# Two matmul layers on one Trainium2 core: x2 of the state rows kept in SBUF, their products moved into the same chunk, and weight-block sums moved from GpSimd to VectorE

## The chip, the core and the metric

One Trainium2 chip, one of its cores. A time is microseconds on the device for one execution; the figure of a kernel is the median of its runs. The engines are TensorE (PE, with its weight loads PEld), VectorE (DVE), ScalarE (ACT) and GpSimd (POOL); SyncE (SP) issues every DMA of this kernel. Each engine works through its own queue in order and waits at semaphores for the others.

## The reference

Inputs are `x` (8 x 8 x 512 x 64) and `state` (8 x 8 x 32 x 64), both float32, and the weights of two layers; the four weight matrices are float64.

```python
# attention both ways, per batch and head
a  = softmax(scale * x @ state.T);   xread = a @ state      # 512 rows per batch
a2 = softmax(scale * state @ x.T);   sread = a2 @ x         # 32 rows per batch: the state rows
x  = concatenate([xread, sread], axis=2)                    # 8 * (512 + 32) = 4352 rows of 512
# first layer: 512 -> 1024 -> 512
h  = x @ w_in;  solu = h * softmax(h);  ln = (solu - mean) / sqrt(var + 1e-6) * g_ln
x2 = ln @ w_out
# second layer: 512 -> 2048 -> 512
h  = x2 @ w_in2;  g = maximum(0.01 * h, h);  out = g @ w_out2
```

## The kernel before

**Precision.** A float32 product is three products of rounded halves: high x high, high x low, low x high. `mm3` (L99) issues them, `split` (L106) makes the halves: ACT rounds the source to the high half, DVE or POOL subtracts it to get the low half. Weights arrive as float64 words and are narrowed by `narrow` (L151): one ACT step (absolute value, L156) and four DVE steps (L157, L158, L161, L164).

**First layer.** Batches 0 to 7 are the 512 rows each of xread; "batch 8" (B) is the 256 state rows of all batches, in two row blocks. For each batch the program does attention, `h1` and `solu_norm` (normalisation), transposes (`tr`, L406) and `x2` (L426), whose result goes by ACT into the buffer `xo` (one buffer) and by DMA to DRAM (`xs`).

**Second layer.** The 2048 features are cut into 8 chunks of 256, the batches into 4 pairs; `second` (L731) walks pair by pair, chunk by chunk. Within a pair `h2` (L625) computes a chunk's hidden values of both batches with seven products instead of eight (block sums S1 to S4 of the weights, differences T1 to T4 of x2), held in three PSUM accumulators X, Z, Y; ACT and DVE combine them, apply the leaky step and split them into `gb` or `gc`. `out2` (L657) multiplies by the second weights. Its call for chunk c stands in the turn of chunk c + 1.
In pair 0 the weights are split once by `split_chunk` (L503), written to DRAM (`w2s`, `wo2s`), and loaded back by the later pairs. For the first weights POOL makes two subtractions of 128x1024 (L510, L521) and the four sums of 128x256 (L516 to L519). The raw words of the next chunk are loaded as soon as DVE has read the old ones.
The state rows go along with pair 0 only: `h8` (L691) their hidden values, `out8` (L708) their output. Their x2 is written to `xs[8]`, loaded back into the tile `misc` (L678), split there (L683), and h8 and out8 of chunk c are issued in the turn of chunk c + 1, the last in the first turn of pair 1.

**What sets the order.** The program text (`PROGRAM`, L815, and `second`) is only a priority: a scheduler places each instruction in its engine's queue by an estimate of its own of when operands, buffers and engines are free. So an edit in one place moves instructions around it on all engines. Buffers are named by tag: the tag `t4` has four rows of 128x1024, which the narrowed weights, the sums and the normalised rows share; `w` has two buffers, which hold the two halves of w_out until the state rows' x2 is done, and then `misc` and the weights of odd chunks.

Of the kernel before, what the change touches and what calls it, by code (L numbers as in the profile page):

```python
# [10 lines left out]
F32 = mybir.dt.float32  # L11
# [4 lines left out]
ALU = mybir.AluOpType  # L16
# [4 lines left out]
P = 128  # L21
# [12 lines left out]
def f32(ap):  # L34
    return ap.bitcast(F32)
# [3 lines left out]
def attn_solu_leaky_kernel(  # L39
# [15 lines left out]
    nc = tc.nc  # L55
    B, H, S, D = x.shape
# [7 lines left out]
    ND = DM // P  # L64
    NF2 = FF2 // P
    ROWS = S + NS
    HALF = 2 * P
# [5 lines left out]
    dr = ctx.enter_context(tc.tile_pool(name="dr", bufs=1, space=DRAM))  # L73

    def slot(tag, shape, dtype, name, bufs=1):
        return sb.tile(shape, dtype, tag=tag, name=name, bufs=bufs)

    def bank(name):
        return ps.tile([P, 512], F32, tag="p1", name=name, bufs=4)
# [14 lines left out]
        return slot("t4", [P, 1024], F32, name, bufs=4)  # L94


    xs = [dr.tile([P, ND, S if j < B else HALF], F32, name=f"xs{j}") for j in range(B + 1)]

    def mm3(o, ah, al, bh, bl, start, stop, more=False):  # L99

# [5 lines left out]
    def split(hi, lo, src):  # L106
        nc.scalar.copy(hi, src)
        nc.vector.tensor_tensor(lo, src, f32(hi), ALU.subtract)  # L108
# [297 lines left out]
    def tr(b, r):  # L406
# [8 lines left out]
        for u in range(NF // 4):  # L415
# [7 lines left out]
            c = slice(r * P, (r + 1) * P)  # L423
            split(t[0][:, 4 * u : 4 * u + 4, c], t[1][:, 4 * u : 4 * u + 4, c], v)

    def x2(b, u):  # L426
        t = ln_t[b]
        pt = bank(f"x2_{b}_{u}")
        nd = 1 if b < B else 2
        nt = S if b < B else HALF  # L430
        for j in range(nd):
            d = slice((nd * u + j) * P, (nd * u + j + 1) * P)
            for f in range(NF):
                mm3(
                    pt[:, j * nt : (j + 1) * nt],
                    w_out_hi[:, f, d], w_out_lo[:, f, d], t[0][:, f, :], t[1][:, f, :],
                    start=(f == 0), stop=(f == NF - 1),
                )
        o = slot("xo", [P, nd, nt], F32, f"xo{b}_{u}", bufs=1)
        nc.scalar.copy(o, pt.rearrange("p (j t) -> p j t", j=nd))  # L440
        nc.sync.dma_start(xs[b][:, nd * u : nd * (u + 1), :], o)

# [25 lines left out]
    def misc():  # L470
        if "misc" not in ph2:
            ph2["misc"] = slot("w", [P, 2, 2, 1024], F32R, "misc", bufs=2)
        return ph2["misc"]

    def w2_tile(p, c):
        w2[p, c] = slot(
            "w" if c % 2 else "sw0", [P, 2, 2, 1024], F32R, f"w2_{p}_{c}", bufs=2 if c % 2 else 1
        )
        return w2[p, c]
# [23 lines left out]
    def split_chunk(c, kind):  # L503
        w = narrow(ph2["raw"][:, kind], f"wn{c}_{kind}")
        if c < NC - 1:
            load_chunk(c + 1, kind)
        if kind == 0:
            t = w2_tile(0, c)
            nc.scalar.copy(t[:, 0, 0], w)
            nc.gpsimd.tensor_tensor(t[:, 0, 1], w, f32(t[:, 0, 0]), ALU.subtract)  # L510
            sm_ = row(f"ws{c}")
            s_ = [sm_[:, i * 256 : (i + 1) * 256].rearrange("p (k f) -> p k f", k=2) for i in range(4)]
            v = w.rearrange("p (h k g f) -> p h g k f", h=2, k=2, g=2)
            a11, a12, a21, a22 = v[:, 0, 0], v[:, 1, 0], v[:, 0, 1], v[:, 1, 1]
            tt = nc.gpsimd.tensor_tensor
            tt(s_[0], a21, a22, ALU.add)  # L516
            tt(s_[1], s_[0], a11, ALU.subtract)
            tt(s_[2], a11, a21, ALU.subtract)
            tt(s_[3], a12, s_[1], ALU.subtract)  # L519
            nc.scalar.copy(t[:, 1, 0], sm_)  # L520
            nc.gpsimd.tensor_tensor(t[:, 1, 1], sm_, f32(t[:, 1, 0]), ALU.subtract)  # L521
            nc.sync.dma_start(w2s[c], f32(t))
        else:
            t = wo2_tile(0, c)
            nc.scalar.copy(t[:, 0], w)
            nc.gpsimd.tensor_tensor(t[:, 1], w, f32(t[:, 0]), ALU.subtract)
            nc.sync.dma_start(wo2s[c], f32(t))
# [97 lines left out]
    def h2(p, c, part, between=None):  # L625
        C = late("C")[:, c % 2]
        g = gtile(c)
        if part == 0:
            hq[p, c] = [bank1(t, f"h{t}{p}_{c}") for t in "XZY"]
        X, Z, Y = hq[p, c]  # L630
        tt = nc.vector.tensor_tensor
        if part == 0:
            prod(X, p, c, "A11", "B11", True)
            nc.scalar.copy(C[:, 0, 0], X)
            prod(Z, p, c, "A12", "B21", True)
            tt(C[:, 0, 0], C[:, 0, 0], Z, ALU.add)  # L636
            prod(X, p, c, "S2", "T2", False)
            nc.scalar.copy(C[:, 1, 0], X)  # L638
            prod(Y, p, c, "S1", "T1", True)
            if between is not None:  # L640
                h8(between)
            prod(X, p, c, "S3", "T3", False)
            nc.scalar.copy(C[:, 1, 1], X)  # L643
            tt(C[:, 1, 1], C[:, 1, 1], Y, ALU.add)  # L644
            leaky(C[:, 0, 0], C[:, 0, 0])
        else:
            prod(X, p, c, "A22", "T4", False)
            leaky(C[:, 0, 1], X)
            nc.scalar.copy(g[:, 0, 0], C[:, 0])
            nc.gpsimd.tensor_tensor(g[:, 1, 0], C[:, 0], f32(g[:, 0, 0]), ALU.subtract)  # L650
            prod(Y, p, c, "S4", "B22", False)
            tt(C[:, 1, 0], C[:, 1, 0], Y, ALU.add)
            leaky(C[:, 1], C[:, 1])
            nc.scalar.copy(g[:, 0, 1], C[:, 1])
            nc.gpsimd.tensor_tensor(g[:, 1, 1], C[:, 1], f32(g[:, 0, 1]), ALU.subtract)

    def out2(p, c, j, rs=(0, 1, 2, 3)):  # L657
        g = gtile(c)
        o = late("oacc")[:, j]
        w = wo2[p, c].rearrange("p h (f d) -> p h f d", f=2)  # L660
        for r in rs:
            t = slice(r * P, (r + 1) * P)
            pt = bank(f"o{p}_{c}_{j}_{r}")
            for f in range(2):
                mm3(
                    pt, g[:, 0, j, f, t], g[:, 1, j, f, t], w[:, 0, f, :], w[:, 1, f, :],
                    start=(f == 0), stop=(f == 1),
                )
            if c == 0:
                nc.scalar.copy(o[:, r, :], pt)  # L670
            else:
                nc.vector.tensor_tensor(o[:, r, :], o[:, r, :], pt, ALU.add)  # L672
            if c == NC - 1:
                rows = out.rearrange("(b t) d -> b t d", t=ROWS)[2 * p + j, :S, :]
                nc.sync.dma_start(rows.rearrange("(p r) d -> p r d", r=NR)[:, r], o[:, r, :])


    def load_x8():  # L678
        nc.sync.dma_start(
            f32(misc()[:, 1, 1]).rearrange("p (k t) -> p k t", k=ND), xs[B]  # L680
        )

    def split_x8():  # L683
        t = misc()[:, 1]
        nc.scalar.copy(t[:, 0], f32(t[:, 1]))
        nc.vector.tensor_tensor(t[:, 1], f32(t[:, 1]), f32(t[:, 0]), ALU.subtract)

    o8 = {}
    g8 = {}
# [41 lines left out]
    def second():  # L731
        ps2.close()
        psb[0] = ctx.enter_context(tc.tile_pool(name="psc", bufs=1, space=PSUM))

        seq = [(p, c) for p in range(NPAIR) for c in range(NC)]
        for i, (p, c) in enumerate(seq):
            prev = seq[i - 1] if i else None
            new = seq[i + 1] if i + 1 < len(seq) else None
            turn = c == NC - 1 and p < NPAIR - 1
            if new and new[0] == 0:  # L740
                split_chunk(c + 1, 0)
            elif new:
                load_w2(*new)
            if turn:
                load_x2(p + 1)
            if not i:
                h2(p, c, 0)
                x2(B, 0)
                h2(p, c, 1)
                x2(B, 1)  # L750
                load_x8()
                split_x8()
                split_chunk(1, 1)
                out2(p, c, 0)
                out2(p, c, 1)
                continue
            h2(p, c, 0, prev[1] if prev[0] == 0 else None)
            if turn:
                diff_x2(p + 1)
                swap_x2("B11", "B21")  # L760
            if i > 1:
                out2(*prev, 0)
            if turn:
                swap_x2("T2")
            h2(p, c, 1)
            if turn:
                swap_x2("T1", "T3")
            if i > 1:
                out2(*prev, 1)
            if turn:  # L770
                swap_x2("T4", "B22")
            if prev[0] == 0:
                out8(prev[1])
            if new and new[0] == 0:
                split_chunk(c + 1, 1)
            elif new:
                load_wo2(*new)
        out2(*seq[-1], 0)
        out2(*seq[-1], 1)
# [66 lines left out]
```

## Time and profile before

| | |
|---|---|
| median of 3 runs | 1186.05 us (1185.74 to 1187.06) |
| the profiled execution | 1186.7 us |
| its span, first to last instruction | 1184.9 us |
| mean granted clock of PE | 0.983 |
| PE busy | 1126.2 us, 95% |
| DVE, ACT, POOL busy | 648.0, 528.5, 348.8 us |
| chain of waits that ended last | PE 83%, DVE 7%, POOL 3%, issue 3%, ACT 2%, DMA 2% |

The second layer starts at 457 us. A row of the timeline has its start, its duration, the engine, the line, the operation with its tiles, and in brackets how long the engine stood idle before it and who released it. A matmul's duration covers more than its share of the engine, since matmuls overlap: the pace is read from start to start.

### The profile page before, as it was taken

What the parts mean: (1) busy time and instruction counts of PE and PEld (TensorE: products, weight loads), DVE (VectorE), ACT (ScalarE), POOL (GpSimd) and SP (SyncE); (2) the same over time, 40 slices, a digit from 0 to 9 for tenths busy, and PEclk for the clock granted to TensorE, in tenths of its full rate; (3) what the DMA queues carried; (4) which work ended last, traced back from release to release, by engine and by line L of the source; (5) the groups of instructions that cost most, each with busy time, mean ns of one, the idle gap of its engine ahead of it and who ended that gap; (6) DMA issues with size and microseconds to landing.
All of it is one profiled execution on the core that took longest, in us unless ns stands there. A gap on an engine that the chain in (4) does not pass through costs nothing.

```text
span 1184.9 us, 14523 instructions
## 1 busy us (share of the span) xinstructions
PE 1126.2 (95%) x5648; PEld 896.7 (76%) x5648; DVE 648.0 (55%) x1015; ACT 528.5 (45%) x811; POOL 348.8 (29%) x241
## 2 busy tenths in 40 slices
PE   4659999999999998989999999999999999999998
PEld 2347677677768867768888888888888888888887
DVE  6988667675675587456665632334723336323434
ACT  3655646655565444554444434233342325342331
POOL 1241112111102032587775222122231313222221
PEclk8869999999999999999999999999999999999999
DMA  9302202202011225646543574435562534634331
GB/s 293 109 1 56 54 30 54 62 13 63 27 54 63 100 113 186 240 152 256 196 169 151 204 273 149 173 119 201 214 247 108 188 132 165 225 139 182 115 134 71
DMA packets 66444, 162.42 MB, mean 137 GB/s; under 512 B 39624, under 2 KB 39624, under 8 KB 57672
## 3 DMA queue, kind: packets, MB, share of 16 engines
q1 hardware_dynamic: 66376, 161.50, 39.2%
q8 instruction: 44, 0.72, 0.2%
q14 instruction: 24, 0.20, 0.1%
HBM read 118.49 MB, written 42.99 MB: 136 GB/s over the span
## 4 chain that ended last, share of the span: by engine, by line
PE 83%; DVE 7%; POOL 3%; issue 3%; ACT 2%; DMA 2%; SPq 1%; POOLq 0%; ACTq 0%; DVEq 0%
PE o L102 10%; PE o L104 10%; PE o L103 10%; PE x L102 5%; PE hX L103 5%; PE hX L104 5%; PE hX L102 5%; PE x L103 5%; PE x L104 5%; PE h L102 3%; PE h L103 3%; PE h L104 3%; PE hY L104 2%; PE hY L102 2%; PE hY L103 2%
## 5 line engine op out<-in xcount | busy, mean ns | idle before, releaser
L672 DVE TENSOR_TENSOR oacc<-oacc,o 128x512 f32<-128x512 f32 x224 | 151.7, 684 | 104.3 <-PE o L104 104.0
L102 PE MATMUL x<-ln,w_out_hi 128*128 128x512 f32 (+1 forms) x288 | 111.3, 387 | 0.9 <-ACT xo L440 0.9
L103 PE MATMUL x<-ln,w_out_hi 128*128 128x512 f32 (+1 forms) x288 | 109.1, 379 | 0.6 <-DVE r L246 0.3
L104 PE MATMUL x<-ln,w_out_lo 128*128 128x512 f32 (+1 forms) x288 | 109.0, 378 | 0.0
L650 POOL TENSOR_TENSOR gc<-C,gc 128x1024 fp32r<-128x1024 f32 x16 | 42.9, 2684 | 197.8 <-issue 141.6
L104 PE MATMUL o<-wo,gb 128*128 128x512 f32 x256 | 99.7, 389 | 0.0
L104 PE MATMUL o<-misc,gc 128*128 128x512 f32 x256 | 99.7, 389 | 0.0
L103 PE MATMUL o<-wo,gb 128*128 128x512 f32 x256 | 99.7, 389 | 0.0
L102 PE MATMUL o<-wo,gb 128*128 128x512 f32 x256 | 99.7, 389 | 0.0
L103 PE MATMUL o<-misc,gc 128*128 128x512 f32 x256 | 99.6, 389 | 0.0
L102 PE MATMUL o<-misc,gc 128*128 128x512 f32 x256 | 99.6, 389 | 0.0
L650 POOL TENSOR_TENSOR gb<-C,gb 128x1024 fp32r<-128x1024 f32 x16 | 40.5, 2533 | 185.3 <-issue 164.8
L598 ACT ACTIVATE C<-C 128x512 f32<-128x512 f32 x64 | 54.1, 846 | 68.3 <-DVE C L636 40.9
L598 ACT ACTIVATE C<-hX 128x512 f32<-128x512 f32 x32 | 19.1, 598 | 145.1 <-PE hX L104 145.0
L102 PE MATMUL hX<-xbT,w 128*128 128x512 f32 x192 | 75.2, 392 | 2.8 <-ACT C L638 1.6
L103 PE MATMUL hX<-xbT,w 128*128 128x512 f32 x192 | 74.9, 390 | 0.0
L104 PE MATMUL hX<-xbT,w 128*128 128x512 f32 x192 | 74.7, 389 | 0.0
L644 DVE TENSOR_TENSOR C<-C,hY 128x512 f32<-128x512 f32 x32 | 21.9, 685 | 93.2 <-ACT C L643 93.2
L102 PEld LDWEIGHTS x<-ln,w_out_hi 128*128 128x128 f32 x288 | 54.2, 188 | 18.1 <-issue 1.9
L102 PE MATMUL h<-sw,a1T 128*128 128x512 f32 x128 | 54.9, 429 | 11.6 <-DVE cf(0, 0)_446 L362 7.9
L636 DVE TENSOR_TENSOR C<-C,hZ 128x512 f32<-128x512 f32 x32 | 22.0, 686 | 77.0 <-PE hZ L104 72.6
L103 PEld LDWEIGHTS x<-ln,w_out_hi 128*128 128x128 f32 x288 | 54.3, 188 | 11.1 <-DVE ln L108 0.9
(718 smaller groups left out, 2711.2 us busy)
## 6 DMA issues: line engine op xcount, KB each, us to landing
w<-w2s SPq DMA_DIRECT2D x24, 2048.0 KB, 7.9
w2s<-w SPq DMA_DIRECT2D x8, 2048.0 KB, 6.8
wo<-wo2s SPq DMA_DIRECT2D x12, 1024.0 KB, 6.8
misc<-wo2s SPq DMA_DIRECT2D x12, 1024.0 KB, 7.1
xs<-xo SPq DMA_DIRECT2D x34, 256.0 KB, 2.4
out<-oacc SPq DMA_DIRECT2D x34, 256.0 KB, 4.9
xn<-in_x SPq DMA_DIRECT2D x32, 256.0 KB, 4.8
raw<-in_moe_w_in SPq DMA_DIRECT2D x8, 1024.0 KB, 5.2
```

What stands on the lines that cost most here:

```text
L102: nc.tensor.matmul(o, ah, bh, start=start, stop=False, **kw)
L103: nc.tensor.matmul(o, ah, bl, start=False, stop=False, **kw)
L104: nc.tensor.matmul(o, al, bh, start=False, stop=stop, **kw)
L598: nc.scalar.activation(o, v, AF.Lrelu)
L636: tt(C[:, 0, 0], C[:, 0, 0], Z, ALU.add)
L644: tt(C[:, 1, 1], C[:, 1, 1], Y, ALU.add)
L650: nc.gpsimd.tensor_tensor(g[:, 1, 0], C[:, 0], f32(g[:, 0, 0]), ALU.subtract)
L672: nc.vector.tensor_tensor(o[:, r, :], o[:, r, :], pt, ALU.add)
```

## The change

1. x2 of the state rows is no longer written to DRAM: ACT copies both halves of it into a tile `x8f` in SBUF (tag `g8`), and `split_x8` splits it from there into `misc`. The load `load_x8` and the tensor `xs[8]` are gone.
2. h8 and out8 of a chunk are issued in the turn of that same chunk: in chunk 0 between and after the two halves of out2, in chunks 1 to 7 in the middle of h2 and at the turn's end. The last ones no longer stand in pair 1.
3. The four sums of each first-weight chunk are made on DVE; the subtractions stay on POOL.

```diff
-    xs = [dr.tile([P, ND, S if j < B else HALF], F32, name=f"xs{j}") for j in range(B + 1)]
+    xs = [dr.tile([P, ND, S], F32, name=f"xs{j}") for j in range(B)]
...
+    x8 = {}
+
     def x2(b, u):
...
-        o = slot("xo", [P, nd, nt], F32, f"xo{b}_{u}", bufs=1)
-        nc.scalar.copy(o, pt.rearrange("p (j t) -> p j t", j=nd))
-        nc.sync.dma_start(xs[b][:, nd * u : nd * (u + 1), :], o)
+        if b == B:
+            if u == 0:
+                x8["f"] = slot("g8", [P, 2, 512], F32, "x8f")
+            nc.scalar.copy(x8["f"][:, u], pt)
+            return
+        o = slot("xo", [P, S], F32, f"xo{b}_{u}", bufs=1)
+        nc.scalar.copy(o, pt)
+        nc.sync.dma_start(xs[b][:, u, :], o)
...
-            tt = nc.gpsimd.tensor_tensor
+            tt = nc.vector.tensor_tensor
             tt(s_[0], a21, a22, ALU.add)
...
-    def load_x8():
-        nc.sync.dma_start(
-            f32(misc()[:, 1, 1]).rearrange("p (k t) -> p k t", k=ND), xs[B]
-        )
-
     def split_x8():
         t = misc()[:, 1]
-        nc.scalar.copy(t[:, 0], f32(t[:, 1]))
-        nc.vector.tensor_tensor(t[:, 1], f32(t[:, 1]), f32(t[:, 0]), ALU.subtract)
+        v = x8["f"].rearrange("p u c -> p (u c)")
+        split(t[:, 0], t[:, 1], v)
...
                 x2(B, 1)
-                load_x8()
                 split_x8()
                 split_chunk(1, 1)
                 out2(p, c, 0)
+                h8(0)
                 out2(p, c, 1)
+                out8(0)
                 continue
-            h2(p, c, 0, prev[1] if prev[0] == 0 else None)
+            h2(p, c, 0, c if p == 0 else None)
...
-            if prev[0] == 0:
-                out8(prev[1])
+            if p == 0:
+                out8(c)
```

What the scheduler makes of it. The line numbers of the changed kernel are 5 to 7 higher from `x2` on. Up to the split of chunk 0 the queues are the same.

DVE's queue where the state rows' first layer ends, before: `wn0_1` and `wn1_0` are narrowed weights (chunk, first or second weights), `e(8, 1)` the second row block's normalised values, `ln8` the low halves after its transposes, `C` and `hZ` hidden values of chunk 0.

```order
L164 SCALAR_TENSOR_TENSOR wn0_1_3815<-raw_3666,wn0_1_3815 128x1024
L376 TENSOR_SCALAR e(8, 1)_3798<-e(8, 1)_3798,c2(8, 1)_3812 128x1024
L158 TENSOR_SCALAR wn1_0_3977<-wn1_0_3977 128x1024
L161 SCALAR_TENSOR_TENSOR wn1_0_3977<-raw_3666,wn1_0_3977 128x1024
L108 TENSOR_TENSOR ln8_3916<-tr8_0_0_3917,ln8_3916 128x4x128
L108 TENSOR_TENSOR ln8_3916<-tr8_0_1_3924,ln8_3916 128x4x128
L164 SCALAR_TENSOR_TENSOR wn1_0_3977<-raw_3666,wn1_0_3977 128x1024
L157 TENSOR_SCALAR wn1_1_4162<-wn1_1_4162 128x1024
```

And now, with the sums `ws1` of chunk 1:

```order
L164 SCALAR_TENSOR_TENSOR wn0_1_3814<-raw_3665,wn0_1_3814 128x1024
L376 TENSOR_SCALAR e(8, 1)_3797<-e(8, 1)_3797,c2(8, 1)_3811 128x1024
L108 TENSOR_TENSOR ln8_3915<-tr8_0_0_3916,ln8_3915 128x4x128
L108 TENSOR_TENSOR ln8_3915<-tr8_0_1_3923,ln8_3915 128x4x128
L158 TENSOR_SCALAR wn1_0_3976<-wn1_0_3976 128x1024
L161 SCALAR_TENSOR_TENSOR wn1_0_3976<-raw_3665,wn1_0_3976 128x1024
L164 SCALAR_TENSOR_TENSOR wn1_0_3976<-raw_3665,wn1_0_3976 128x1024
L523 TENSOR_TENSOR ws1_3986<-wn1_0_3976 128x256
L525 TENSOR_TENSOR ws1_3986<-wn1_0_3976 128x256
L524 TENSOR_TENSOR ws1_3986<-ws1_3986,wn1_0_3976 128x256
L157 TENSOR_SCALAR wn1_1_4157<-wn1_1_4157 128x1024
```

The two subtractions of the first row block moved ahead of two steps of the narrowing, and the sums follow its last step.

ACT's queue at the same place is nearly unchanged; this is how it stands now (`wn1_1` the absolute value of chunk 1's second weights, `xo7_2` a copy of x2 of batch 7, `hX0_0` the copy of chunk 0's first product):

```order
L532 CAST wo2_0_0_3821<-wn0_1_3814 128x1024
L156 ACTIVATE wn1_1_4157<-raw_3665 128x1024
L447 COPY xo7_2_3955<-x2_7_2_3930 128x512
L107 CAST ln8_3915<-tr8_1_0_3958 128x4x128
L107 CAST ln8_3915<-tr8_1_1_3965 128x4x128
L641 COPY C_3696<-hX0_0_3995 128x512
```

Before, the copy of batch 7 stood behind that of `hX0_0`; the absolute value stood ahead of the casts as it does now.

DVE's queue at the end of chunk 0, now: `ws2` are the sums of chunk 2, `misc` with `x8f` the low half of the state rows' x2.

```order
L659 TENSOR_TENSOR C_3696<-C_3696,hY0_0_3997 128x512
L523 TENSOR_TENSOR ws2_4289<-wn2_0_4279 128x256
L525 TENSOR_TENSOR ws2_4289<-wn2_0_4279 128x256
L524 TENSOR_TENSOR ws2_4289<-ws2_4289,wn2_0_4279 128x256
L526 TENSOR_TENSOR ws2_4289<-wn2_0_4279,ws2_4289 128x256
L108 TENSOR_TENSOR misc_4154<-x8f_4083,misc_4154 128x1024
L157 TENSOR_SCALAR wn2_1_4402<-wn2_1_4402 128x1024
```

Before, nine rows stood between that C and the subtraction of x2: the narrowing of two weights and the first sum of chunk 1's hidden values; now only the four sums stand between. The first sum waits for POOL, which subtracts the high half from the narrowed weights of chunk 1: their row of `t4` becomes `ws2`. On PE, h8 of chunk 0 moved from behind chunk 1's first four products to behind the first 24 matmuls of chunk 0's outputs, and out8 of chunk 0 from chunk 2's start to chunk 1's.

## Rows read from the trace of the kernel before

**Rows 1.** Page, part 4, shares of the span by engine.

```profile
PE 83%; DVE 7%; POOL 3%; issue 3%; ACT 2%; DMA 2%; SPq 1%; POOLq 0%; ACTq 0%; DVEq 0%
```

**Rows 2.** Table by stretches: length, busy us (instructions) per engine, clock, DMA share, GB/s.

```profile
446.00:480.00 34.00, 29.70 (x172) 25.88 (x171) 21.62 (x24) 17.00 (x23) 12.51 (x9) 0.95 0.55 186
480.00:545.00 65.00, 56.52 (x259) 45.70 (x258) 37.12 (x37) 33.94 (x46) 48.45 (x26) 0.97 0.60 223
545.00:1176.00 631.00, 631.00 (x2851) 525.15 (x2850) 275.97 (x368) 234.21 (x308) 200.45 (x90) 1.00 0.46 170
```

**Rows 3.** Timeline of PE, 446 to 545 us: matmuls it waited for.

```profile
447.06 0.50 PE L102 MATMUL x<-ln,w_out_hi 128*128 128x512 f32 x1 [0.92 <-ACT xo L440]
456.82 0.66 PE L419 MATMUL tr<-ident,e(8, 1)_3798 128*128 128x128 f32 x4 [2.99 <-DVE ln L108]
495.00 0.50 PE L102 MATMUL hX<-xbT,w 128*128 128x512 f32 x1 [1.21 <-ACT C L634]
499.60 0.39 PE L103 MATMUL h<-misc,w 128*128 128x256 f32 x1 [1.46 <-DVE misc L686]
506.20 0.50 PE L104 MATMUL hZ<-xbB,w 128*128 128x512 f32 x1 [1.70 <-POOL w L510]
512.76 0.72 PE L104 MATMUL o<-wo,g 128*128 128x512 f32 x1 [2.03 <-POOL g L706]
525.52 0.50 PE L102 MATMUL hX<-xbT,w 128*128 128x512 f32 x1 [1.64 <-ACT C L638]
```

**Rows 4.** Table by stretches, 514 to 516 us, behind two of the gaps.

```profile
514.00:516.00 2.00, 2.00 (x6) 1.52 (x6) 1.52 (x2) 1.20 (x2) 2.00 (x2) 0.50 0.00 0
```

**Rows 5.** Timeline of PE without a gap: start to start.

```profile
464.40 0.39 PE L102 MATMUL hX<-xbT,w 128*128 128x512 f32 x1
465.76 0.28 PE L102 MATMUL x<-ln,w_out_hi 128*128 128x256 f32 x1
...
471.51 0.40 PE L102 MATMUL hX<-xbT,w 128*128 128x512 f32 x1
```

**Rows 6.** Timeline of DVE and POOL, 525 to 533 us.

```profile
525.96 1.23 DVE L161 SCALAR_TENSOR_TENSOR wn<-raw,wn 128x1024 uint32<-128x1024 uint32 x1
527.22 3.31 DVE L164 SCALAR_TENSOR_TENSOR wn<-raw,wn 128x1024 uint32<-128x1024 uint32 x1
...
529.41 3.39 POOL L521 TENSOR_TENSOR w<-ws,w 128x1024 fp32r<-128x1024 f32 x1
```

**Rows 7.** Timeline of ACT, POOL and SP, 480 to 487 us.

```profile
480.09 1.05 ACT L509 CAST w<-wn 128x1024 fp32r<-128x1024 f32 x1 [2.77 <-PE x L103]
...
481.21 2.41 POOL L510 TENSOR_TENSOR w<-wn,w 128x1024 fp32r<-128x1024 f32 x1 [1.42 <-ACT w L509]
...
486.48 0.32 SPq L679 DMA_DIRECT2D misc<-xs  x1
```

**Rows 8.** The tile ws: count, duration min/median/max in ns, starts.

```profile
L516 POOL TENSOR_TENSOR ws<-wn x8: 732/739/1050, 428.4 to 610.6; 128x256 f32<-128x256 f32 x8
```

**Rows 9.** Timeline of SP and ACT, 439 to 460 us.

```profile
439.00 0.34 SPq L522 DMA_DIRECT2D w2s<-w  x1
...
446.42 0.59 ACT L440 COPY xo<-x 128x512 f32<-128x512 f32 x1 [2.11 <-DMA xs<-xo]
...
451.58 0.38 SPq L498 DMA_DIRECT2D raw<-in_moe_w_out  x1
...
456.59 1.17 ACT L156 ACTIVATE wn<-raw 128x1024 f32<-128x1024 f32 x1 [2.50 <-DMA raw<-in_moe_w_out]
457.67 1.06 ACT L107 CAST ln<-tr 128x512 fp32r<-128x512 f32 x2
459.31 0.59 ACT L634 COPY C<-hX 128x512 f32<-128x512 f32 x1 [0.58 <-PE hX L104]
```

**Rows 10.** Chain of waits in order of time: start, us, what.

```profile
439.43 6.89 DMA xs<-xo
```

**Rows 11.** Page, part 6: count, KB each, median us from issue to landing.

```profile
xs<-xo SPq DMA_DIRECT2D x34, 256.0 KB, 2.4
```

## The prediction

> **What bounds the kernel now.** I read the chain of waits first: 83% of the span is TensorE (PE) and no other engine has more than 7% [rows 1]. So I asked where PE is not busy, with the table by stretches [rows 2]. From 545 to 1176 us PE is busy 631.00 of 631.00 us, so nothing that the change does to chunks 3 to 7 and to the later passes can shorten the kernel; it can only lengthen it. All that can be won lies between 446 and 545 us, where the state rows end and the first three chunks of the second layer start: 34 - 29.70 = 4.30 us idle up to 480, 65 - 56.52 = 8.48 us idle up to 545, together 12.8. The waits themselves, with who ends them, are in [rows 3]; two more of 0.4 us are not shown. Then the clock: the mean grant is 0.95 and 0.97 in the two stretches [rows 2], and in one of the bad windows it is 0.50, that is 1.2 GHz instead of 2.4 [rows 4]. 34 x 0.05 and 65 x 0.03 are 1.7 and 2.0 us lost to it, once after the 2.99 us gap and once after the 1.70 and 2.03 us gaps. At most 12.8 + 3.7 = 16.5 us can be won, and PE does the same matmuls as before: 6 of 512 columns take 1.36 us (0.227 each), 48 of 256 columns 5.75 us (0.12 each) [rows 5]. So the forecast is a sum of waits, old against new.
>
> **A fact that prices the new sums.** A VectorE (DVE) operation on two SBUF operands takes 1.23 us alone, but 3.31 us when POOL's subtraction stands beside it; POOL's next one then takes 3.39 us [rows 6] instead of 2.41 [rows 7]. They do not share; one waits for the other, and they take turns when both are queued. The Trainium skill says it as a rule ("SBUF — State Buffer", section "SBUF: two separate sides"): a DVE instruction with two SBUF inputs and a GpSimd instruction that reads SBUF lock each other out of a shared port pair for the whole instruction. The trace agrees (3.31 against 1.23 us). By that rule the four sums, moved to DVE, still stand against POOL; were each to run at its own duration, the time would be that of the first rival below.
> One sum of 128x256 costs POOL 0.74 us [rows 8]; DVE has no row of that size. Its 128x1024 operation takes 1.23 us, a quarter of that is 0.31, and it should not be slower than POOL: bounds 0.31 and 0.74. I take 0.35, near the row of the same engine. Four sums: 1.4 us more on DVE per chunk, at least 4 x 0.74 = 3.0 less on POOL.
>
> **First place: the end of the state rows and chunk 0.** In chunk 0's split DVE makes the sums while POOL subtracts; one POOL subtraction falls between them (DVE's last sum waits for it), and DVE then waits for POOL's second one before it splits T2. I put the state rows' normalisation 1.6 us later by this. Against it, POOL reaches the end of its split 3 us sooner (its four sums are gone), so the 2 MB write of the split weights, issued at 439.00, goes at about 436.0. The copy of x2 into its buffer stood idle for 2.11 us up to 446.42 [rows 9], for a write queued behind that one, which took 6.89 us to land [rows 10]; this wait goes. The two nearly cancel: I put the second row block's normalisation 0.2 us earlier, and with it the raw load of chunk 1's second weights, which DVE releases: 451.4 instead of 451.58 [rows 9].
> What changes is what stands behind what. DVE's two subtractions of the first block now come ahead of two steps of the narrowing, so the transposes no longer wait 2.99 us: I put idle times of 0.05 and 0.2 in place of 0.92, 0.38 and 2.99. PE starts chunk 0 at 453.2, 4 us earlier (456.82 and four transposes in the trace), and has done 12 matmuls by 453.2 + 2.7 = 455.9. There it needs ScalarE's (ACT's) copy of the first product. ACT stands in order behind the absolute value of the raw weights, which waits for their landing: 451.4 + 5.0 = 456.4 (451.58 to 456.59 in the trace [rows 9]), then 1.1 for it, 0.5 for a copy of x2, 1.05 for two casts, 0.55 for the copy itself: 459.6. In the trace that copy starts at 459.31 [rows 9]. So the wait moves to the third product: 459.6 - 455.9 less the 0.15 by which a matmul's record outlasts its issue (0.39 against 0.227), 3.55 us of idle, and 0.2 at the fifth, for ACT's next copy. New idle 0.05 + 0.2 + 3.55 + 0.2 = 4.0 against 4.3. A gap of 3.55 is longer than the one that brought the clock down before, so I charge the same 1.7 us. Gain of the first place: 0.3 us.
>
> **Second place: from the end of the state rows' products (480.05, called E) to the end of chunk 2.** Removed: the two writes of x2 to DRAM and the load back, issued at 486.48 [rows 7], the waits 1.21, 1.46, 1.70, 2.03, 1.64 [rows 3] and 0.44. The products of the state rows (h8) now stand behind the first 24 matmuls of chunk 0's outputs: PE comes to them at E + 24 x 0.227 + 0.35 = E + 5.8. They need the low half of x2, which DVE subtracts, and its queue has the four sums of chunk 2 ahead. ACT starts at E + 0.04; four casts of 1.05 [rows 7] and a copy of 0.6 give the high half of x2 by E + 4.9, so ACT is not the last. POOL's first subtraction runs E + 1.15 to 3.55, the next to 5.9, the third after it. The first sum writes a row that the first subtraction reads, so it can start at 3.6; the second subtraction has the pair by then, so it runs 5.9 to 6.2; POOL's third takes 6.2 to 8.6; the other three sums run to 9.5, the subtraction of x2 (1.2) to 10.7. PE waits 10.7 - 5.8 = 4.9, in idle as the trace counts it 4.8 us. The gap is long enough for the clock again: 1.7.
> Then the outputs of the state rows (o8): ACT's and POOL's pieces come 7 to 8 us after h8, since POOL subtracts the next chunk's weights ahead of them: 0.7 us of idle, where the trace has 2.03. Chunk 1's o8, split by the scheduler round two products: 0.25. New idle 4.8 + 0.7 + 0.25 = 5.75 against 8.48, clock 1.7 against 2.0. Gain of the second place: 3.0 us.
>
> **Hidden.** From chunk 3 on DVE has 1.4 us more per chunk of some 26 us, and POOL less; in 545 to 1176 DVE is busy 276 and POOL 200 of 631 us [rows 2]. PE covers it; were that cover gone, it would cost up to 1.4 us in each of five chunks. Weights of even chunks come free earlier, since their last reader moved up a chunk.
> Sum: 0.3 + 3.0 = 3.3, taken as 3.5 for the small steps. The profiled execution took 1186.7 us (span 1184.9), 0.65 above the median; from the median, 1186.05 - 3.5 = 1182.5 us.
>
> **Rivals.**
> 1. The sums run beside POOL at their own duration, or DVE gets all four through between two subtractions. Then they end at E + 5.05, the subtraction of x2 at 6.3, PE waits 0.4 instead of 4.8 and the clock stays: 4.4 + 1.7 more, 1176.4 us. For it: the sums are short, and no row shows one on DVE. Against it: [rows 6], where DVE's operands lie in SBUF as theirs do.
> 2. No change. One more POOL subtraction (2.4 us) gets in between the sums, and the raw weights land 1 us later: 3.4 us back, 1186 us. For it: both places hang on turns between two queues that I can only infer. Against it: POOL has nothing ready after its third subtraction until h8 is done.
> 3. Slower. The load of chunk 1's second weights lands late, and ACT, in order behind it, holds the copy that frees PE's first accumulator. Each us of delay costs PE one us; from 3.5 us on (landing after 459.9) the kernel is slower. The transfer queued behind the 2 MB write landed after 6.89 us [rows 10] where 2.4 is the median [rows 11], 4.5 late; the same lateness here, and a second table load or clock drop of 1.7, give 1182.5 + 4.5 + 1.7 = 1188.7 us. For it: this wait is the longest of the first place, with nothing else to do for PE. Against it: the big write leaves at 436 and is done by 443.
>
> **How the numbers follow.** Forecast 0.48 (its own range, with either clock drop missing or a sum at 0.74, 1179 to 1184.5), rival 1 0.20, rival 2 0.20, rival 3 0.12. 0.2% is 2.4 us, about what a measurement of this kernel can tell from no change. Faster: three quarters of the forecast's share, all of rival 1 and a little of rival 2, 0.58; slower: rival 3 and a little of rival 2, 0.14; the rest, 0.28, the same. The range runs from rival 1 to rival 3: 1176 to 1188.5.
>
> **What would show it.** Right: PE's first gap of the second layer stands at chunk 0's third product and is ended by an ACT copy, at 459 to 460; a second one at h8 of chunk 0, some 6 us after the state rows' products end, ended by the subtraction of x2 on DVE, with sums of more than 1 us beside POOL; none of the old waits at 495 to 525; PE full from chunk 3 on. Wrong: sums of 0.35 us throughout and no gap at h8 (rival 1); a gap at the third product that ends after 460 (rival 3); gaps in chunks 3 to 7, which I hold for excluded.

## The result, and the profile after

The changed kernel takes 1196.82 us (median of 3 runs, 1195.38 to 1197.66), the kernel before 1186.05: a ratio of 1.0086, 95% interval 1.0072 to 1.0100. It is slower by 10.8 us, where 3.5 us faster was forecast, and outside the range of 1176 to 1188.5. The profiled execution took 1195.4 us, its span is 1193.6.

The table by stretches after (columns as in [rows 2]):

```profile
446.00:480.00 34.00, 30.08 (x174) 26.07 (x173) 21.68 (x29) 16.70 (x23) 8.22 (x6) 0.95 0.53 176
480.00:545.00 65.00, 59.47 (x283) 49.49 (x282) 47.22 (x49) 37.40 (x50) 36.66 (x16) 0.95 0.56 210
545.00:600.00 55.00, 50.71 (x237) 42.30 (x237) 43.15 (x50) 22.15 (x29) 26.89 (x12) 0.97 0.51 192
600.00:700.00 100.00, 95.78 (x447) 79.82 (x447) 61.24 (x69) 37.31 (x48) 40.97 (x17) 0.98 0.46 172
700.00:800.00 100.00, 99.75 (x440) 82.28 (x439) 38.35 (x52) 35.05 (x48) 24.01 (x10) 1.00 0.49 180
```

Read the difference of the first two numbers, PE's idle time. In the two stretches that I worked out it is 3.92 and 5.53 us (forecast: 4.0 and 5.75; before: 4.30 and 8.48). Behind them, where PE was full before, it is 4.29, 4.22 and 0.25. The timeline of PE names the waits:

```profile
458.53 0.50 PE L102 MATMUL hX<-xbT,w 128*128 128x512 f32 x1 [3.77 <-ACT C L641]
489.43 0.58 PE L103 MATMUL h<-misc,w 128*128 128x256 f32 x1 [4.85 <-DVE misc L108]
500.14 0.50 PE L104 MATMUL o<-wo,g 128*128 128x512 f32 x1 [0.19 <-POOL g L708]
513.82 0.50 PE L104 MATMUL o<-misc,g 128*128 128x512 f32 x1 [0.48 <-POOL g L708]
556.02 0.50 PE L102 MATMUL hX<-xbT,w 128*128 128x512 f32 x1 [2.51 <-ACT C L645]
584.21 0.50 PE L102 MATMUL hX<-xbT,w 128*128 128x512 f32 x1 [1.78 <-ACT C L645]
613.99 0.50 PE L102 MATMUL hX<-xbT,w 128*128 128x512 f32 x1 [1.78 <-ACT C L645]
633.10 0.50 PE L102 MATMUL o<-misc,g 128*128 128x512 f32 x1 [2.45 <-DVE oacc L679]
```

(From `h8` on the line numbers are only 2 higher than before: L706 is now L708.) The waits of [rows 3] are gone. The first four rows were forecast, the last four were not; three of them stand in chunks 3, 4 and 5, the last at chunk 5's outputs for the state rows. At four of the gaps the granted clock falls from 1.00 to 0.50, that is from 2.4 to 1.2 GHz, for 3 to 7 us: those of 3.77, 4.85 and 2.45 us and the one of 1.78 us at 584 us. At the gap of 2.51 us and the other one of 1.78 us it stays at 1.00, so the length of a gap alone does not tell. Here are the stretches behind the gaps of 4.85, 2.51 and 1.78 us (the clock is the third column from the end):

```profile
489.00:494.00 5.00, 4.57 (x23) 4.57 (x24) 4.96 (x7) 0.00 (x0) 0.00 (x0) 0.55 0.76 316
556.00:561.00 5.00, 4.98 (x22) 4.09 (x23) 4.90 (x5) 1.69 (x3) 2.03 (x1) 1.00 0.48 183
584.00:589.00 5.00, 4.79 (x14) 3.86 (x15) 4.90 (x6) 1.87 (x4) 2.30 (x1) 0.67 0.51 186
```

The account: idle from 446 to 800 us is 3.92 + 5.53 + 4.29 + 4.22 + 0.25 = 18.2 against 12.8, so 5.4 more. Clock: 34 x 0.05 + 65 x 0.05 + 55 x 0.03 + 100 x 0.02 = 8.6. Of this, 1.4 us fall inside the gap of 4.85 us itself (mean clock 0.72), where PE does nothing and a low clock costs nothing. So it is 7.2 against 3.7, 3.5 more. Together that is 8.9 us, and the span grew by 8.7. The account is good to a microsecond or so: the clock is rounded to 0.01, and before 200 us, where the queues are the same, PE happened to be busy 160.58 instead of 159.13 us.

**Where the new waits come from.** PE waits for ACT's second copy of hX; ACT stands behind the leaky step of C, which waits for DVE's addition of hZ. The timeline of chunk 3 after, PE's last matmul into hZ first, then POOL, DVE and ACT:

```profile
547.53 0.39 PE L104 MATMUL hZ<-xbB,w 128*128 128x512 f32 x1
...
542.87 2.41 POOL L528 TENSOR_TENSOR w<-ws,w 128x1024 fp32r<-128x1024 f32 x1
545.24 2.85 POOL L662 TENSOR_TENSOR gb<-C,gb 128x1024 fp32r<-128x1024 f32 x1
548.05 2.84 POOL L533 TENSOR_TENSOR misc<-wn,misc 128x1024 fp32r<-128x1024 f32 x1
...
544.12 1.71 DVE L157 TENSOR_SCALAR wn<-wn 128x1024 f32<-128x1024 f32 x1 [2.26 <-ACT wn L156]
546.35 2.29 DVE L158 TENSOR_SCALAR wn<-wn 128x1024 uint32<-128x1024 uint32 x1
549.16 2.81 DVE L161 SCALAR_TENSOR_TENSOR wn<-raw,wn 128x1024 uint32<-128x1024 uint32 x1
552.50 1.21 DVE L164 SCALAR_TENSOR_TENSOR wn<-raw,wn 128x1024 uint32<-128x1024 uint32 x1
553.81 0.42 DVE L523 TENSOR_TENSOR ws<-wn 128x256 f32<-128x256 f32 x1
554.15 0.68 DVE L643 TENSOR_TENSOR C<-C,hZ 128x512 f32<-128x512 f32 x1
...
554.87 0.63 ACT L605 ACTIVATE C<-C 128x512 f32<-128x512 f32 x1 [2.77 <-DVE C L643]
555.40 0.57 ACT L645 COPY C<-hX 128x512 f32<-128x512 f32 x1
```

And before, DVE at the same place:

```profile
547.05 0.69 DVE L636 TENSOR_TENSOR C<-C,hZ 128x512 f32<-128x512 f32 x1 [2.10 <-PE hZ L104]
548.97 0.69 DVE L157 TENSOR_SCALAR wn<-wn 128x1024 f32<-128x1024 f32 x1 [1.23 <-ACT wn L156]
549.70 0.69 DVE L158 TENSOR_SCALAR wn<-wn 128x1024 uint32<-128x1024 uint32 x1
550.43 1.23 DVE L161 SCALAR_TENSOR_TENSOR wn<-raw,wn 128x1024 uint32<-128x1024 uint32 x1
```

Before, DVE idles 2.10 us, adds hZ half a microsecond after PE's last matmul into it has started, and narrows the next weights afterwards at 0.69 and 1.23 us a step. After, the narrowing and the first sum stand ahead of the addition, their steps take 1.71, 2.29 and 2.81 us between POOL's subtractions, and the addition starts 6.6 us behind that matmul. All of this came forward. The first step into the buffer of chunk 4's first weights is ACT's rounding; POOL's subtraction follows it. Before, ACT waits for the product `h` of the state rows, the buffer's last reader, and POOL starts at 553.71 us:

```profile
552.58 1.05 ACT L509 CAST w<-wn 128x1024 fp32r<-128x1024 f32 x1 [2.64 <-PE h L104]
553.71 2.40 POOL L510 TENSOR_TENSOR w<-wn,w 128x1024 fp32r<-128x1024 f32 x1 [5.92 <-ACT w L509]
```

After, that product stands a turn earlier, ACT rounds at 537.20 us without waiting, and POOL follows:

```profile
540.50 2.41 POOL L517 TENSOR_TENSOR w<-wn,w 128x1024 fp32r<-128x1024 f32 x1
```

The order of DVE's queue in the changed kernel has the narrowing of chunk 5's first weights ahead of chunk 3's hZ, as the timeline has it (rows of the output additions, oacc and oacc8, left out):

```
L157 TENSOR_SCALAR wn5_0_4806<-wn5_0_4806 128x1024
L158 TENSOR_SCALAR wn5_0_4806<-wn5_0_4806 128x1024
L161 SCALAR_TENSOR_TENSOR wn5_0_4806<-raw_3665,wn5_0_4806 128x1024
L164 SCALAR_TENSOR_TENSOR wn5_0_4806<-raw_3665,wn5_0_4806 128x1024
L523 TENSOR_TENSOR ws5_4816<-wn5_0_4806 128x256
L643 TENSOR_TENSOR C_3696<-C_3696,hZ0_3_4628 128x512
```

The wait of 2.45 us at 633 us has another holder: DVE's first difference for pair 1 stands ahead of the output addition (L679) that PE waits for. It takes 3.40 us, with POOL's subtractions beside it:

```profile
629.05 3.40 DVE L557 TENSOR_TENSOR T<-xin 128x1024 f32<-128x1024 f32 x1 [3.16 <-POOL w L517]
```

This is read from the trace; no run takes this wait away by itself.

### The profile page after: what moved, and what is told of

Its sections match the earlier page's. It is cut to its first block, busy times and chain, and to the rows that moved or that the text cites. A ratio compares the mean times of both kernels' runs of the same rounds, so it can differ in the third digit from the quotient of the medians.

```text
span 1193.6 us, 14521 instructions
## 1 busy us (share of the span) xinstructions
PE 1130.8 (95%) x5648; PEld 897.1 (75%) x5648; DVE 680.6 (57%) x1047; ACT 529.1 (44%) x811; POOL 313.5 (26%) x209
## 4 chain that ended last, share of the span: by engine, by line
PE 72%; DVE 11%; issue 6%; ACT 3%; POOL 3%; DMA 3%; SPq 1%; POOLq 0%; ACTq 0%; DVEq 0%
PE o L104 8%; PE o L103 8%; PE o L102 8%; PE x L102 5%; PE x L103 4%; PE x L104 4%; PE hX L102 4%; PE hX L103 4%; PE hX L104 4%; PE h L104 2%; PE h L103 2%; PE h L102 2%; PE hY L103 2%; PE hY L102 2%; PE hY L104 2%
## 5 line engine op out<-in xcount | busy, mean ns | idle before, releaser
L679 DVE TENSOR_TENSOR oacc<-oacc,o 128x512 f32<-128x512 f32 x224 | 152.0, 685 | 101.3 <-PE o L104 100.9
L657 POOL TENSOR_TENSOR gc<-C,gc 128x1024 fp32r<-128x1024 f32 x16 | 39.9, 2494 | 206.8 <-issue 133.7
L651 DVE TENSOR_TENSOR C<-C,hY 128x512 f32<-128x512 f32 x32 | 22.0, 687 | 99.3 <-ACT C L650 99.3
L659 DVE TENSOR_TENSOR C<-C,hY 128x512 f32<-128x512 f32 x32 | 21.9, 686 | 76.3 <-PE hY L104 76.3
```

## The experiments

Theory A: h8 and out8 in the new turn free the weights' buffers half a chunk earlier; POOL's subtractions and the narrowing of the next weights come forward with them; DVE's addition of hZ falls behind a narrowing that POOL stretches. Theory B, the rival: the four sums on DVE make it late. Theory C, added when theory A's account of the old turn failed: in the old turn the sums stand on DVE waiting for a row of `t4`. Each run is timed beside the kernel before on the same chip. There were three chips, and the kernel before took 1186.36, 1186.80 and 1186.31 us on them; differences between runs below carry that half microsecond.

| run | parts of the change | median, us | ratio to before, 95% |
|---|---|---|---|
| x8_in_sbuf_only | 1 | 1186.39 | 0.9993 to 1.0010 |
| sums_on_pool | 1, 2 | 1191.18 | 1.0031 to 1.0056 |
| sums_on_dve_only | 3 | 1206.36 | 1.0155 to 1.0183 |
| old_turn | 1, 3 | 1202.73 | 1.0119 to 1.0156 |
| the change | 1, 2, 3 | 1196.82 | 1.0072 to 1.0100 |
| hz_first | 1, 2, 3 | 1187.44 | 1.0000 to 1.0017 |
| thin_low_halves | 1, 2, 3 | 1184.89 | 0.9981 to 0.9999 |
| leaky_behind | 1, 2, 3 | 1188.63 | 1.0009 to 1.0027 |
| leaky_h8_last | 1, 2, 3 | 1187.72 | 0.9999 to 1.0016 |
| leaky_raw | 1, 2, 3 | 1208.54 | 1.0174 to 1.0202 |
| old_turn_raw | 1, 3 | 1204.23 | 1.0136 to 1.0163 |
| old_turn_sums_later | 1, 3 | 1189.12 | 1.0013 to 1.0032 |
| ordered | 1, 2, 3 | 1186.45 | 0.9985 to 1.0007 |

### The parts apart

**sums_on_pool.** On the changed kernel:

```diff
-            tt = nc.vector.tensor_tensor
+            tt = nc.gpsimd.tensor_tensor
```

> The changed kernel with its four sums back on POOL (parts 1 and 2 of the change alone). Theory A (the new turn of h8 and out8 brings the split of the next weights forward, so that on DVE the addition of hZ stands behind the narrowing of the next chunk, and the narrowing is stretched by POOL's subtractions): PE still waits for ACT's second copy of hX in chunks 3, 4 and 5, 1.3 to 2.5 us each, and the time is 1190 to 1198 us. Theory B (the sums on DVE are what makes DVE late): these waits are gone, 545 to 640 us is full, and the time is 1180 to 1185 us.

Measured 1191.18 us: theory A's waits are there without any sum on DVE, at 1.47, 1.25 and 1.25 us instead of 2.51, 1.78 and 1.78. Part 1 alone (x8_in_sbuf_only, below) has none of them. So the new turn makes them, and the sums make them 0.5 to 1.0 us longer.

**sums_on_dve_only.** The opposite edit, on the kernel before.

> The kernel before with the four sums on DVE (part 3 alone). Theory A: PE stays full from 545 us on, the waits between 480 and 545 us stay much as before, 1183 to 1187 us. Theory B: waits for ACT's copies of hX behind DVE's addition of hZ in chunks 3 to 5, 2 us each, 1192 us or more.

Measured 1206.36 us, the second worst of all. Theory A's forecast fails, and theory B's place is wrong too: the waits behind hZ's addition are not there, others are. The waits of PE in this run (us in total, times, longest):

```profile
PE o L102 <- DVE oacc L672: 9.0, 7, 1.9
PE hX L102 <- ACT C L634: 5.4, 2, 3.5
PE hY L102 <- DVE C L644: 5.1, 5, 2.3
```

DVE's own waits from 480 to 640 us, and its timeline, show why:

```profile
DVE ws L516 <- POOL w L510: 25.2, 5, 8.5
```

```profile
560.03 2.60 DVE L516 TENSOR_TENSOR ws<-wn 128x256 f32<-128x256 f32 x1 [3.58 <-POOL w L510]
...
564.33 0.68 DVE L644 TENSOR_TENSOR C<-C,hY 128x512 f32<-128x512 f32 x1
```

The first sum writes the row of `t4` that the first weights of the chunk before leave, and POOL's subtraction is its last reader. While POOL made the sums this cost nothing, since they stood behind that subtraction in its own queue. On DVE it is a wait of 25 us in five chunks, with hY's addition and the accumulators behind it. This is theory C.

**old_turn.** On the changed kernel, the calls of h8 and out8 as before:

```diff
-                h8(0)
                 out2(p, c, 1)
-                out8(0)
                 continue
-            h2(p, c, 0, c if p == 0 else None)
+            h2(p, c, 0, prev[1] if prev[0] == 0 else None)
...
-            if p == 0:
-                out8(c)
+            if prev[0] == 0:
+                out8(prev[1])
```

> The changed kernel with h8 and out8 of a chunk back in the turn of the next chunk (parts 1 and 3 alone: x2 of the state rows in SBUF, sums on DVE). Theory A: no wait of PE over 0.5 us after 545 us, no half clock there, and none at h8 of chunk 0; 1178 to 1185 us. Theory B: the waits in chunks 3 to 5 stay, 1190 us or more.

Measured 1202.73 us, with the same 9.0 and 5.1 us of waits as sums_on_dve_only. Theory A is right only that the waits behind hZ and the one at h8 go; its forecast of the time misses by 18 us, since it knew nothing of theory C.

**x8_in_sbuf_only.** The old turn and the sums on POOL together.

> Part 1 of the change alone: x2 of the state rows in SBUF, h8 and out8 in the old turn, sums on POOL. Theories A and C have nothing to say against it: DVE's queue stays as before from chunk 1 on, so no wait appears after 545 us; the wait for the low half of x2 at h8 (1.5 us) goes; 1183 to 1187 us.

Measured 1186.39 us, no change, at the upper end of what was expected. The wait of 1.46 us at h8 is gone, but ACT's copy ahead of it is waited for 2.63 instead of 1.21 us: the wait moved.

### The new turn: place and contention

**hz_first.** On the changed kernel, one rule of order on DVE, no wait on a result:

```diff
-        w = narrow(ph2["raw"][:, kind], f"wn{c}_{kind}")
+        with behind(*([("hz", 0, c - 2)] if kind == 0 and c > 3 else [])):
+            w = narrow(ph2["raw"][:, kind], f"wn{c}_{kind}")
```

> The changed kernel with one rule of order added and nothing else: on DVE the narrowing of the first weights of chunks 4 to 7 is queued behind the addition of hZ of the chunk two before (order of issue only, no wait on a result). If the place behind the narrowing is what makes PE wait for ACT's second copy of hX in chunks 3, 4 and 5, these three waits (6.1 us) and the half clock behind them (some 2 us) go, the wait of 2.4 us at 633 us and the two of the first places stay, and the time is 1187 to 1191 us. If DVE is short of time as such, waits of the same sum turn up at hY or at the outputs and the time stays at 1194 us or more.

Measured 1187.44 us, 9.4 us less than the changed kernel. PE is busy 55.00 of 55 us from 545 to 600, and of the waits, 1.0 us at out8 apart, only those that were to stay are left:

```profile
PE h L103 <- DVE misc L699: 4.8, 1, 4.8
PE hX L102 <- ACT C L651: 3.7, 2, 3.4
PE o L102 <- DVE oacc L689: 2.4, 1, 2.4
```

```profile
548.83 0.69 DVE L653 TENSOR_TENSOR C<-C,hZ 128x512 f32<-128x512 f32 x1 [2.10 <-PE hZ L104]
549.44 1.91 DVE L157 TENSOR_SCALAR wn<-wn 128x1024 f32<-128x1024 f32 x1
```

DVE has the same work and the same POOL beside it. The place in its queue costs the 9.4 us: 6.1 us of waits, some 1.7 of the clock behind one of them (55 x 0.03); the remaining 1.6 were not traced.

**thin_low_halves.** On the changed kernel, for both halves of g (from chunk 2 of pair 0 on this kernel leaves out 480 of 512 columns of the low halves):

```diff
-            nc.gpsimd.tensor_tensor(g[:, 1, 1], C[:, 1], f32(g[:, 0, 1]), ALU.subtract)
+            k = slice(0, 32 if p == 0 and c > 1 else S)
+            nc.gpsimd.tensor_tensor(g[:, 1, 1, :, k], C[:, 1, :, k], f32(g[:, 0, 1, :, k]), ALU.subtract)
```

> The changed kernel, with DVE's queue in the same order, but POOL makes only 32 of 512 columns of the low halves of the hidden values in pair 0 from chunk 2 on (the rest of them keeps what stood there), so that two of POOL's subtractions per chunk nearly vanish. Theory A (narrowing steps stretched beside POOL): the steps of 1.7, 2.3 and 2.8 us shrink to their 0.7 to 1.2, the addition of hZ comes some 3 us earlier, PE's waits in chunks 3 to 5 fall below 0.5 us and the time is 1185 to 1190 us. Rival: the place alone (the addition behind four steps of narrowing at their own durations) is late enough; waits over 1 us stay, 1193 us or more.

Measured 1184.89 us. DVE's order is that of the changed kernel, yet the waits in chunks 3 to 5 shrink to 0.50, nothing and nothing. Only part of the mechanism is as expected: L157 takes 1.04 and L161 1.21 us, but L158 still 2.57, now beside L533, and the addition starts 4.6 instead of 6.6 us behind the matmul. Two microseconds less are enough to spare PE. Place and contention act together: with less of the contention the same place does little harm, and hz_first ends the waits with the contention left.

**leaky_behind.** On the changed kernel, so that ACT has nothing that waits for DVE ahead of its copies of hX:

```diff
-            leaky(C[:, 0, 0], C[:, 0, 0])
...
-            leaky(C[:, 0, 1], X)
+            nc.scalar.copy(C[:, 0, 1], X)
+            leaky(C[:, 0], C[:, 0])
```

> The changed kernel with the leaky step of the first quarter of a chunk's hidden values made together with the second quarter's (ACT copies X first, one step of 128x1024 in place of two of 128x512), so that ACT's copies of hX no longer stand behind a step that waits for DVE. Theory A: DVE's addition of hZ is as late as in the changed kernel, but PE no longer waits for it: the three waits of 1.8 to 2.5 us in chunks 3 to 5 and their half clock go, 1186 to 1190 us, unless hY or the outputs' accumulators wait for DVE next. If instead DVE is short of time as such, PE waits as long at hY or at the outputs and the time stays at 1195 us or more.

Measured 1188.63 us. The addition of hZ is as late as ever (6.7 us behind its matmul), and PE no longer minds: 0.2 us at that copy. The path PE, ACT, leaky step, DVE is shown from its middle. A wait it does not touch grew:

```profile
PE h L103 <- DVE misc L108: 6.2, 1, 6.2
```

### The sums' row

**old_turn_raw.** On old_turn:

```diff
-            sm_ = row(f"ws{c}")
+            sm_ = f32(ph2["raw"][:, 0].rearrange("p f e -> p (f e)")[:, :1024])
...
             nc.sync.dma_start(w2s[c], f32(t))
+            if c < NC - 1:
+                load_chunk(c + 1, kind)
```

> old_turn with the four sums written into the first 4 KB of the raw words just narrowed, in place of a fifth user of the four rows of t4; the raw load of the next first weights is issued behind their last reader. Theory C (with h8 and out8 in the old turn the sums hold DVE, since the row they write is freed by a POOL subtraction of the chunk before, and hY's addition and the outputs' accumulators stand behind them): DVE no longer idles for POOL ahead of the sums (22 us in old_turn), PE's waits for the accumulators and for hY (9.0 and 5.1 us) fall below 1 us each from 545 us on; 1180 to 1188 us. Rival: DVE is short of time as such, or the sums' collision with POOL is enough; the waits stay and the time is 1197 us or more.

Measured 1204.23 us. It tells nothing of theory C: DVE's wait for POOL is gone, but the raw load now starts later, is waited for, and holds ACT in its place (the tile of the raw words, waits before its users):

```profile
  DMA raw<-in_moe_w_in: 14.2, 6
```

**old_turn_sums_later.** On old_turn, order alone:

```diff
+            with behind(*([("hy", 0, c - 2)] if c > 2 else [])):
                 tt(s_[0], a21, a22, ALU.add)
...
```

> old_turn with one rule of order added: on DVE the sums of chunks 3 to 7 are queued behind the last addition of hY of the chunk in whose time they fall. Theory C (the sums stand on DVE waiting for a row that a POOL subtraction frees, and hold hY's addition and the outputs' accumulators): DVE no longer idles for POOL ahead of them, PE's waits for the accumulators (9.0) and for hY (5.1) fall below 2 us together, and the time falls from 1202.7 to 1183 to 1188 us. If the sums cost DVE time it does not have, or POOL's turns beside them are the harm, the time stays above 1195 us.

Measured 1189.12 us, 13.6 us less, a microsecond above what was expected. DVE waits for POOL ahead of the sums once, not five times (tile ws), and the waits of PE for the accumulators and hY fall from 14.1 to 4.7 us, not below 2:

```profile
  POOL w L517: 8.5, 1
```

```profile
PE o L102 <- DVE oacc L689: 3.0, 4, 0.7
PE hY L102 <- DVE C L661: 1.7, 1, 1.7
```

Theory C holds in the main: against x8_in_sbuf_only, where POOL makes the sums, the same four sums on the same engine cost 16.3 us or 2.7, by where they stand.

**leaky_raw.** The edit of old_turn_raw on leaky_behind.

> leaky_behind with the sums written into the raw words just narrowed. By theory C the sums of chunk 2 no longer stand and wait ahead of the subtraction of x2, so the wait at h8 of chunk 0 (6.2 us) falls below 1 us; the narrowing of each chunk's first weights starts later, since their load waits for the sums' readers. 1180 to 1185 us; if ACT, which takes the raw words in order, then holds PE's copies of hX while a load is on its way, 1188 us or more.

Measured 1208.54 us, the slowest. The wait at h8 does fall, from 6.2 to 0.2 us, as theory C has it; the late raw loads cost far more (waits for ACT's copies of hX and for the accumulators of 12.3 and 10.2 us).

### Towards a faster kernel

**leaky_h8_last.** On leaky_behind, h8(0) one line down, behind out2(p, c, 1).

> leaky_behind with h8 of chunk 0 behind the second half of that chunk's outputs, not the first: 24 matmuls, 5.4 us, more ahead of it. If the wait of 6.2 us at h8 is only DVE's subtraction of x2 coming late (behind the sums of chunk 2, which wait for POOL to free their row), PE's wait there is 1 us at most, its half clock goes too, out8 of chunk 0 stands behind chunk 1's first products, and the time is 1181 to 1184 us. If the products of chunk 1 wait for the same weights or queues, the wait moves and the time stays at 1187 to 1189 us.

Measured 1187.72 us, 0.9 less than leaky_behind. The wait at h8 fell as expected, but out8 came to wait for POOL and hY for DVE:

```profile
PE o L104 <- POOL g L708: 3.8, 2, 3.0
PE hY L102 <- DVE C L651: 1.8, 1, 1.8
PE h L103 <- DVE misc L108: 1.1, 1, 1.1
```

**ordered.** On hz_first, three more rules of order:

```diff
-        with behind(*([("hz", 0, c - 2)] if kind == 0 and c > 3 else [])):
+        with behind(*([("hz", 0, c - 2)] if kind == 0 and c > 3 else []), *([("cx", 0, 0)] if (c, kind) == (1, 1) else [])):
...
+            with behind(*([("x8")] if c == 2 else [])):
                 tt(s_[0], a21, a22, ALU.add)
...
-                diff_x2(p + 1)
...
                 out2(*prev, 0)
+            if turn:
+                with behind(("ol", *prev, 0)):
+                    diff_x2(p + 1)
```

> The changed kernel with four rules of order: on DVE the narrowing of chunks 4 to 7 behind hZ's addition (as in hz_first), the sums of chunk 2 behind the subtraction of the state rows' x2, the differences for pair 1 behind the outputs of the turn; on ACT the absolute value of chunk 1's second weights behind the third copy of hX of chunk 0. By my account of the waits, the gaps of 3.8 us (chunk 0's third product), 4.8 us (h8), 6.1 us (chunks 3 to 5) and 2.4 us (633 us) all fall below 1 us, and with them most of the half clock: 1174 to 1181 us. If one of them only moves, 1182 us or more.

Measured 1186.45 us: no better than before, and within what was expected if waits only move. The gap of 4.85 us at h8 fell to 1.1 and the clock of the profiled execution is 1.00 in every stretch from 446 us on, but waits of 1.1 to 1.8 us stand in eight places. The twelve times fall into two groups, 1182.9 to 1185.2 us at a mean clock of 0.984 to 0.990, and 1187.7 to 1188.6 us at 0.979 to 0.981. The profile (1183.11 us) is of the first group, so where the clock falls in the second is open. No version that does all the work beats the kernel before beyond its interval.

## Why the prediction was wrong

**First place: right.** Forecast idle 4.0, measured 3.92. The gap stands at the third product and is ended by ACT's copy, which stands behind the absolute value of the raw words; these landed at 455.41 (forecast 456.4), so rival 3 did not come. PE reached its third product a microsecond early as well (its twelfth matmul is issued by 454.6 us, forecast 455.9), so the gap kept its length: both follow from a head start of 1.3 us that stands before the first moved instruction (ACT's first rounding of chunk 0 at 426.94 us, before at 428.26). The clock took 1.7 us, as forecast. ACT's timeline after:

```profile
455.41 1.14 ACT L156 ACTIVATE wn<-raw 128x1024 f32<-128x1024 f32 x1 [4.34 <-DMA raw<-in_moe_w_out]
...
457.88 0.60 ACT L641 COPY C<-hX 128x512 f32<-128x512 f32 x1
```

**Second place: right.** Forecast 5.75, measured 5.53; h8's wait 4.85 against 4.8, with DVE's sums and POOL's subtractions taking turns as reckoned:

```profile
482.24 2.61 DVE L523 TENSOR_TENSOR ws<-wn 128x256 f32<-128x256 f32 x1 [8.51 <-POOL w L517]
484.78 2.57 DVE L525 TENSOR_TENSOR ws<-wn 128x256 f32<-128x256 f32 x1
...
488.15 1.22 DVE L108 TENSOR_TENSOR misc<-x8f,misc 128x1024 fp32r<-128x1024 f32 x1
```

With the sums on POOL (sums_on_pool) h8 waits 1.1 us, which agrees: the gap is made of the two engines' turns. The clock reads 65 x 0.05 = 3.3 us lost there, but 1.4 of it lie inside the gap; behind it, from 489.43 to 493.50 us, it is 0.50 and costs 2.0 us, where 1.7 was forecast. A sum that meets nobody takes 0.42, from start to start 0.34, where 0.35 was taken. Two small slips did no harm: three sums at 0.35 behind 8.6 end at 9.65, not 9.5, and POOL's four sums cost more than 4 x 0.74 = 3.0, since [rows 8] shows the first of them alone (0.74, 0.75, 1.19 and 1.72 us in chunk 1).

**Hidden: this step failed.** It said that from chunk 3 on DVE has 1.4 us more work per chunk, that "PE covers it", and that gaps there were "excluded". It priced added work against a busy share (276 of 631 us), and neither bears on it: in sums_on_pool DVE has none of this work, and the waits are there. What decides is which instruction stands ahead of hZ's addition in DVE's queue, and when POOL's subtractions run. The step even named the cause, "Weights of even chunks come free earlier, since their last reader moved up a chunk", and gave it no cost (it holds for odd chunks too: POOL's subtractions for chunks 4 to 7 start 13.2, 11.1, 7.4 and 5.4 us earlier). What the runs showed in its place: 8.5 us of waits and the clock behind two of them. hz_first shows the price of the place in the queue: 9.4 us, 1196.8 less 1187.4, for an order that stood in DVE's queue to be read before the run, in a part of it that I did not look at.

**The bound of that step was wrong too.** "Up to 1.4 us in each of five chunks" covers work, not waits: sums_on_dve_only lost 20 us by the same sums. In the changed kernel most of that is gone (10.8 us of DVE's waits for POOL ahead of the sums, in two places, against 25.2 in five), since POOL's subtraction, which frees the row, comes earlier there. So part 2 of the change cures most of what part 3 does alone, and does a harm of its own. That is why the parts do not add up: 4.8 us for parts 1 and 2, 16.4 for 1 and 3, 10.8 for all.

**The sign.** Up to chunk 3 the forecast gain is there. Chunk 3's first product starts at 545.04 us, before at 544.06, but the state rows' matmuls of chunk 2 (24 x 0.12 + 12 x 0.227 = 5.6 us) are then already done: 4.6 us ahead, 1.3 of them from before chunk 0. The 3.3 that are left are the 0.3 + 3.0 of the prediction's sum. The four waits behind it, 8.5 us, and the clock behind those, 3.7 us, turned the sign. hz_first still has the fourth wait and the clock behind it, 2.45 + 1.7 us; less these its 1187.4 would be 1183.3 us, near the forecast 1182.5. That is an estimate; no run shows it. My slower rival stood in the first place; none stood where I held PE for covered.

## What to carry to other kernels

An instruction that waits costs what stands behind it in its queue, not its own duration: here the sums cost little on POOL, whose own subtraction frees their row, and on DVE, waiting for that subtraction, they held everything behind them (20 us in sums_on_dve_only). A buffer that comes free earlier starts its next user earlier, so ask what that user now stands ahead of, and whom it meets. Where a scheduler sets the order, read the whole queue of every engine that the change touches, the stretches that look covered above all.

## What the hardware showed

A DVE step with a single SBUF operand is stretched beside POOL as well: L158 takes 0.69 us alone and 2.29 in the rows of chunk 3 above, where it ends 0.6 us after POOL's subtraction; I had counted on this for two operands only. The Trainium skill ("SBUF — State Buffer", section "Who interferes with whom") has it: tensor_scalar can enter a mode of DVE that takes the port pair it shares with GpSimd. The traces agree, 2.29 against 0.69 us.
